# Order of work in the prologue, the first slice, the last attention and the closing sum of a fused attention and MLP kernel

## The chip, the cores and the metric

The kernel runs on one core of a Trainium2 chip. The metric is the device time of one execution in microseconds (us). TensorE is PE in the rows, VectorE DVE, ScalarE ACT, GpSimd POOL, and SyncE SP; "PEld" is TensorE's loading of weights, and a name with a q behind it (ACTq, SPq) is an engine's own queue of DMA issues.

## The reference

```python
def _attn_ref(q, k, v, lam):            # q, k, v: (4, 8, 768, 64)
    block = 64
    ...
    for b in range(nb):
        sl = slice(b * block, (b + 1) * block)
        qb, kb, vb = (q[:, :, sl], k[:, :, sl], v[:, :, sl])
        intra = np.einsum('bhic,bhjc->bhij', qb, kb) * Dmask[None]
        intra = np.einsum('bhij,bhjd->bhid', intra, vb)
        inter = np.einsum('bhid,bhde->bhie', qb * lam_pow[None], kv_state)
        out[:, :, sl] = intra + inter
        kb_dec = kb * rev_pow[None]
        kv_state = lam_block[None, :, None, None] * kv_state + np.einsum('bhsd,bhse->bhde', kb_dec, vb)
    return out

def _moe_ref(x, w_in, w_out):           # x: (3072, 512), d_ff 2048
    h = x @ w_in
    r = np.maximum(h, 0.0)
    g = r * r
    return g @ w_out
```

An attention with a decaying state, in order of the tokens, gives 3072 rows of 512; two matrix products with a squared ReLU between them follow.

## The kernel before

**Tiles and stages.** The tokens are cut into 24 chunks of 128 (`NT`), four batches of six; four chunks make a group of 512 tokens (`G`), so there are six groups. Of each group the MLP's hidden layer is made in 16 slices of 128 features (`NF`). The program runs through a prologue (chunks 0 to 3: loads, masks, their attention), then the first group's 16 slices beside the attention of chunks 4 to 7, then the second group's slices beside chunks 8 to 15, then the groups 2 and 3 in eight steps `quad` beside chunks 16 to 23, their gathering (`gather_all(2, ...)`), and the same for groups 4 and 5 (`quad_all`, `gather_all(4, ...)`). The order of the instructions on every engine is the order of the calls in the program: each engine has one queue and works it off in that order, waiting on semaphores.

**Two parts per number.** Products are made of a high and a low part (types of 32 bits): `wh`, `wl` for weights, `xh`, `xl` for activations, `gh`, `gl` for the squared hidden layer. A product of two numbers is three matmuls: high by high, low by high, high by low.

**A chunk of attention.** `scores(t)` makes k by q on TensorE, `masked(t)` multiplies them by the mask on VectorE (two instructions), `within(t, ...)` multiplies the result with v on TensorE, `news` and `faded` make the state's update, `update` writes the state `kv` (ScalarE up to chunk 3, VectorE behind), `before(t, ...)` adds the product of q and the state, `split` and the function that it returns write `xh` (ScalarE) and `xl` (VectorE). `prep_k` and `prep_q` multiply k and q by powers of lambda on POOL. In the prologue these calls are written out one by one.

**The weights of the first group.** The weights come as 64-bit words in 17 units (`NLOT`; unit u holds slice u of the first matrix and slice u - 1 of the second). A unit goes through a row of steps: `wload(u)` (SP, two DMAs into `raw`, of which there are two buffers), `first_hi(u)` (ScalarE, L120, absolute value into `A`, also two buffers) and `first_lo(u)` (ScalarE, L125), then on VectorE `clamp(u)` L133, `shift(u)` L137, `sign(u)` L144 and `rounded(u)` L150 (an add, which frees `raw`), then `upper(u)` (ScalarE, L156, writes `wh`) and `lower(u)` (VectorE, L159, writes `wl` and frees `A`). `turn(u, ...)` is a copy of one element on POOL that puts POOL's queue behind a step of VectorE. Slice f of the first group calls `hidden(0, f, ...)` first (12 matmuls, L518, which need unit f), then the steps of unit f + 2 (clamp to rounding add) and the last steps of unit f + 1, then `square` (ScalarE: a ReLU and two squares, L525 to L528) and `rest` (VectorE, L533, the remainder `gl` of slice f), and at last on TensorE `project` of the slice before, which needs `gh`, `gl` of that slice and unit f. The body of that loop:

```python
        h = hidden(0, f, *xs_of[0])
        if f < 3:
            ...
        else:
            if u_ < NLOT:
                for op in (clamp, shift, sign):
                    op(u_)
            if f > 3:
                upper(u_ - 1)
            lower(u_ - 1)
            ...
            if u_ < NLOT:
                rounded(u_)
        wload(u_ + 2)
        ...
        rest(0, f, h, gh)
        ...
        if step == 1 and f > 1:
            masked(t)
```

**Last attention.** In `quad(n)` seven products (`product(n, i, ...)`, six matmuls each, L691) run with one attention among them (`go`, L446 and others). `go` multiplies q by the old state, puts a one-element copy on ScalarE (`mark`, L462) behind it, on which the second half waits, runs what the caller gave it as `ahead` and the next chunk's scores, and then the rest. In the last step (n = 7) there is no next chunk, so nothing runs between the two halves.

**Closing sum.** `gather_all` multiplies the gathered rows into seven banks; in its last round it adds them in pairs on VectorE (`add`, L214) and stores four quarters of the output from ScalarE's queue (`put_out`, L1046).

Of the kernel before, what the change touches and what calls it, by code (L numbers as in the profile page):

```python
# [15 lines left out]
P = 128  # L16
# [9 lines left out]
G = 4  # L26
# [9 lines left out]
def body(ctx: ExitStack, tc: tile.TileContext, qT, kT, kvq, lam, w, out):  # L36
# [476 lines left out]
    def hidden(m, f, xh, xl):  # L513
        h = ps_h.tile([P, N], F32, name="h")
        k = 0
        for wt, x in ((wh, xh), (wl, xh), (wh, xl)):
            for kt in range(KT):
                nc.tensor.matmul(  # L518
                    h, wt[:, f, kt * P : (kt + 1) * P], x[:, kt], start=k == 0, stop=k == 11
                )  # L520
                k += 1
        return h
# [263 lines left out]
    def quad(n, prev, far_, last_):  # L786
# [9 lines left out]
        def attention():  # L796
            if n and n in FOLDED:
                fold_whole(FOLDED[n])
            go(t, None if last else t + 1, a_at)
            if t + 2 < NT:  # L800
                load_qk(t + 2)
                load_kv(t + 2)
            if n == NQ - 2:
                move(11, by_half(io.tile([P, 2 * DM], F32, name="qk_sb")[:, 0:DM]))
            if not last:
                scale_q(t + 1)
            if n == 3:
                E[6] = wk.tile([P, N], F32, name="kept", tag="a")
# [27 lines left out]
        product(n, 3, pb, False, False)  # L836
# [207 lines left out]
    def put_out(m, par, two, half, x):  # L1044
        o_ = out[m * G * C : (m + 2) * G * C].rearrange("(r s w p) d -> p r s w d", r=2, s=2, w=2)
        store = lambda: nc.scalar.dma_start(out=o_[:, :, two, par, half * 2 * P : (half + 1) * 2 * P], in_=x.rearrange("p (r d) -> p r d", r=2))  # L1046
# [5 lines left out]
    def gather_all(m, after):  # L1052
        for par in range(2):
# [8 lines left out]
            for n in range(NQ):  # L1062
                q = par * NQ + n
                end = n == NQ - 1
                for i in range(7):
# [21 lines left out]
                    if i == 3:  # L1087
                        add(u3, banks[3], u2)
                        add(o12[0][:, 0], banks[2], u3)
                        put_out(m, par, 1, 1, o12[0][:, 0])  # L1090
# [101 lines left out]
    low[1] = split(1, o[1])  # L1192
    scores(3, ps_acc, "acc")
# [3 lines left out]
    att(2, ps_a, "att")  # L1197
    news(2, u[2])
    faded(2, u[2])
    before(2, o[2], True, False)  # L1200
    update(2, u[2])
    within(2, o[2], False, True)
# [23 lines left out]
    for f in range(NF):  # L1226
        t, step, u_ = G + f // 4, f % 4, f + 2
        h = hidden(0, f, *xs_of[0])
        if f < 3:
# [9 lines left out]
            sign(u_)  # L1239
            if f != 1:  # L1240
                rounded(u_)
        else:
            if u_ < NLOT:
                for op in (clamp, shift, sign):
                    op(u_)
            if f > 3:
                upper(u_ - 1)
            lower(u_ - 1)
            if u_ - 1 < NF:
                turn(u_ - 1, False)  # L1250
            if u_ < NLOT:
                rounded(u_)
        wload(u_ + 2)
        if f == 3:
            low[G]()
# [15 lines left out]
        if f == 1:  # L1271
            rounded(u_)
        if step == 1 and f > 1:
# [176 lines left out]
```

## Time and profile before

| what | us |
|---|---|
| median of three runs (575.71 to 576.35) | 576.0 |
| the profiled execution | 575.8 |
| its span in the profile | 574.0 |
| TensorE busy (98%) | 565.0 |
| VectorE busy (77%) | 441.9 |
| ScalarE busy (52%) | 299.4 |
| POOL busy (17%) | 95.4 |

The times in the rows count from the span's start. A row of the timeline has start, length, engine, line and operation, output and inputs with their tile names, and in brackets how long the engine sat idle ahead of it and what released it. TensorE's matmuls overlap: a matmul of 128x512 has 0.39 us in its row, though the next starts 0.23 later. The first group's slices lie between 25.7 and 127 us, the last attention of `quad` at 324 to 328, the closing sum behind 565.

### The profile page before, as it was taken

To read this page: it belongs to the slowest core of one execution; us is meant where nothing else is said; L and a number is where in the kernel's file an instruction comes from. 1 tells how busy PE (TensorE), PEld (TensorE's weight loads), DVE (VectorE), ACT (ScalarE), POOL (GpSimd) and SP (SyncE) were. 2 spreads that over 40 slices of the span, in tenths; PEclk is the share of its full clock that TensorE was granted. 3 is DMA by queue.
4 is the path that set the end of the run, shared out by engine and by line. 5 is a ranking of instruction groups with operands and counts; after the bars stand their busy time and mean duration, and the time that the engine had idled before them with its cause. 6 is when DMAs were issued, how large, how long until landed. Compare 5 with 4: busy or idle time off the path is not lost.

```text
span 574.0 us, 13432 instructions
## 1 busy us (share of the span) xinstructions
PE 565.0 (98%) x5308; PEld 492.8 (86%) x5308; DVE 441.9 (77%) x732; ACT 299.4 (52%) x524; POOL 95.4 (17%) x107
## 2 busy tenths in 40 slices
PE   9998999999999999999999999999999999999996
PEld 7886888888888888888888799999988888999996
DVE  6899999987787667777773799696865457997933
ACT  4677877834555556566665775153423234541610
POOL 5430321432322233222433000000000000000000
PEclk9999999999999999999999999999999999999999
DMA  8947485427599887599999776799588766766863
GB/s 293 351 150 271 147 276 193 155 103 265 184 353 361 271 264 269 179 306 376 385 372 352 247 223 218 205 297 338 188 267 246 190 196 196 234 212 211 288 202 107
DMA packets 87325, 142.69 MB, mean 249 GB/s; under 512 B 7776, under 2 KB 40544, under 8 KB 87264
## 3 DMA queue, kind: packets, MB, share of 16 engines
q1 hardware_dynamic: 82624, 136.61, 72.2%
q10 hardware_dynamic: 4640, 5.24, 2.5%
q8 instruction: 42, 0.69, 0.5%
q14 instruction: 19, 0.16, 0.1%
HBM read 106.96 MB, written 31.46 MB: 241 GB/s over the span
## 4 chain that ended last, share of the span: by engine, by line
PE 87%; DMA 5%; DVE 5%; ACT 1%; issue 1%; SPq 1%; DVEq 0%; ACTq 0%
PE h L691 19%; PE acc L1035 16%; PE h L518 12%; PE att L1035 8%; PE att L691 8%; PE acc L549 4%; PE h L1035 4%; PE acc L554 4%; PE acc L550 4%; PE acc L446 2%; DMA lent<-in_qT 1%; PE att L446 1%; DMA ws<-parts 1%; DMA kv_sb<-in_kvq 1%; DMA qk_sb<-in_qT 1%
## 5 line engine op out<-in xcount | busy, mean ns | idle before, releaser
L691 PE MATMUL h<-wh,ring 128*128 128x512 f32 x320 | 87.1, 394 | 0.0
L691 PEld LDWEIGHTS h<-wh,ring 128*128 128x128 f32 x320 | 59.2, 188 | 13.3 <-DVE kv_sb L214 0.4
L1035 PE MATMUL acc<-folds,wh 128*128 128x256 f32 x384 | 70.5, 283 | 0.0
L1035 PEld LDWEIGHTS acc<-folds,wh 128*128 128x128 f32 x384 | 59.9, 192 | 0.0
L1007 ACT CAST wh<-sums 128x1024 fp32r<-128x1024 f32 x32 | 33.6, 1050 | 45.9 <-DVE sums L214 15.2
L1035 PE MATMUL acc<-folds,wl 128*128 128x256 f32 x192 | 54.3, 283 | 0.0
L549 PE MATMUL acc<-wh,gh 128*128 128x512 f32 x128 | 50.3, 393 | 0.0
L554 PE MATMUL acc<-wh,gl 128*128 128x512 f32 x128 | 49.9, 390 | 0.0
L550 PE MATMUL acc<-wl,gh 128*128 128x512 f32 x128 | 49.9, 390 | 0.0
L691 PE MATMUL h<-wl,ring 128*128 128x512 f32 x160 | 49.3, 390 | 0.0
L214 DVE TENSOR_TENSOR wl<-sums,wh 128x1024 fp32r<-128x1024 f32 x37 | 45.1, 1220 | 2.8 <-ACT wh L1007 2.8
L525 ACT ACTIVATE h<-h 128x512 f32<-128x512 f32 x32 | 18.7, 583 | 43.1 <-PE h L518 43.1
L1035 PEld LDWEIGHTS acc<-folds,wl 128*128 128x128 f32 x192 | 36.9, 192 | 0.0
L507 POOL TENSOR_TENSOR kvd<-kv,qpow 128x256 f32<-128x256 f32 x27 | 20.7, 766 | 96.7 <-DVE kv L214 79.6
L518 PE MATMUL h<-xh,wh 128*128 128x512 f32 x128 | 36.1, 403 | 0.0
L518 PE MATMUL h<-xh,wl 128*128 128x512 f32 x128 | 34.5, 392 | 1.5 <-DVE wl L159 1.5
L533 DVE TENSOR_TENSOR gl<-h,gh 128x512 fp32r<-128x512 f32 x32 | 22.0, 686 | 17.9 <-ACT h L528 17.9
L691 PEld LDWEIGHTS h<-wl,ring 128*128 128x128 f32 x160 | 30.0, 188 | 6.4
L691 PE MATMUL att<-wh,ring 128*128 128x512 f32 x128 | 34.3, 390 | 0.0
L518 PE MATMUL h<-xl,wh 128*128 128x512 f32 x128 | 34.3, 390 | 0.0
L518 PEld LDWEIGHTS h<-xh,wl 128*128 128x128 f32 x128 | 23.9, 188 | 7.2 <-DVE wl L159 1.9
L886 ACT ACTIVATE h<-h 128x512 f32<-128x512 f32 x16 | 9.3, 581 | 38.3 <-PE h L691 27.2
(267 smaller groups left out, 1423.9 us busy)
## 6 DMA issues: line engine op xcount, KB each, us to landing
folds<-wt SPq DMA_DIRECT2D x128, 256.0 KB, 3.8
ring<-ws SPq DMA_DIRECT2D x112, 256.0 KB, 4.1
raw<-in_w SPq DMA_DIRECT2D x30, 512.0 KB, 4.3
kv_sb<-in_kvq SPq DMA_DIRECT2D x22, 512.0 KB, 6.0
ws<-parts SPq DMA_DIRECT2D x32, 256.0 KB, 4.6
qk_sb<-in_kT SPq DMA_DIRECT2D x22, 256.0 KB, 4.6
qk_sb<-in_qT SPq DMA_DIRECT2D x22, 256.0 KB, 5.0
out_x<-qk_sb ACTq DMA_DIRECT2D x16, 256.0 KB, 5.1
```

What stands on the lines that cost most here:

```text
L214: lambda o, x, y, op=op: V.tensor_tensor(out=o, in0=x, in1=y, op=op)
L446: nc.tensor.matmul(o[h][r, p * D : (p + 1) * D], x, y, start=(h, r.start) not in begun, stop=end, skip_group_check=True,)
L507: nc.gpsimd.tensor_tensor(out=kvd, in0=d, in1=qpow[:, :, D - 1 : D].broadcast_to([P, NPR, D]), op=ALU.mult)
L518: nc.tensor.matmul(h, wt[:, f, kt * P : (kt + 1) * P], x[:, kt], start=k == 0, stop=k == 11)
L525: nc.scalar.activation(h, h, AF.Relu)
L533: V.tensor_tensor(out=gl, in0=r, in1=gh.bitcast(F32), op=ALU.subtract)
L549: nc.tensor.matmul(accs[m][i], gh[:, cs], wh[:, j], start=f == 0, stop=False)
L550: nc.tensor.matmul(accs[m][i], gh[:, cs], wl[:, j], start=False, stop=False)
L554: nc.tensor.matmul(accs[m][i], gl[:, cs], wh[:, j], start=False, stop=end)
L691: nc.tensor.matmul(bank, x[:, part_, kt], t[:, q + kt], start=start and z == 0, stop=stop and z == 5, skip_group_check=True,)
L1007: nc.scalar.copy(o_, x)
L1035: nc.tensor.matmul(bank[:, r * 2 * P : (r + 1) * 2 * P], x, y, start=k == 0 and r == 0 and z == 0, stop=k == NQ - 1 and z == 2, skip_group ...
```

## The change

- **Prologue.** The masked product of chunk 2 (`within(2, ...)`) now comes ahead of the scores of chunk 3; it opens the bank, and `before(2, ...)` closes it.
- **First group.** In slices 4 to 15 `hidden` takes the matmuls of `wl` last. In slices 0 to 5 the rounding add of unit f + 2 comes behind the remainder of slice f, and with it the load of unit f + 4; in slice 1 the sign step too. In slice 3 the lower weights of unit 4 come first, a marker stands behind unit 5's sign step, and `low[G]` comes behind the rounding add.
- **Last attention.** Product 3 of the last `quad` runs between the two halves of the attention.
- **Closing sum.** The first quarter is made by a ScalarE copy of bank 3 and a POOL add of `c` (bank 2 plus `u2`), and is stored from SP's queue; VectorE has one add less.

```diff
@@ hidden
-        for wt, x in ((wh, xh), (wl, xh), (wh, xl)):
+        order = ((wh, xh), (wl, xh), (wh, xl))
+        if m == 0 and f > 3:
+            order = order[0], order[2], order[1]
+        for wt, x in order:
@@ quad, attention()
-            go(t, None if last else t + 1, a_at)
+            if last:
+                go(t, None, a_at, ahead=(lambda: product(n, 3, pb, False, False), lambda: None))
+            else:
+                go(t, t + 1, a_at)
@@ quad
-        product(n, 3, pb, False, False)
+        if not last:
+            product(n, 3, pb, False, False)
@@ put_out
-    def put_out(m, par, two, half, x):
+    def put_out(m, par, two, half, x, queue=nc.scalar):
-        store = lambda: nc.scalar.dma_start(...)
+        store = lambda: queue.dma_start(...)
@@ gather_all
                     if i == 3:
                         add(u3, banks[3], u2)
-                        add(o12[0][:, 0], banks[2], u3)
-                        put_out(m, par, 1, 1, o12[0][:, 0])
+                        if m == 4 and par:
+                            nc.scalar.copy(o12[0][:, 0], banks[3])
+                            nc.gpsimd.tensor_tensor(out=o12[0][:, 0], in0=o12[0][:, 0], in1=c, op=ALU.add)
+                            put_out(m, par, 1, 1, o12[0][:, 0], nc.sync)
+                        else:
+                            add(o12[0][:, 0], banks[2], u3)
+                            put_out(m, par, 1, 1, o12[0][:, 0])
@@ prologue
+    att(2, ps_a, "att")
+    within(2, o[2], True, False)
     scores(3, ps_acc, "acc")
     prep_q(3)
     prep_k(3)
     masked(3)
-    att(2, ps_a, "att")
     news(2, u[2])
     faded(2, u[2])
-    before(2, o[2], True, False)
+    before(2, o[2], False, True)
     update(2, u[2])
-    within(2, o[2], False, True)
@@ the loop over the first group's slices
-            sign(u_)
             if f != 1:
-                rounded(u_)
+                sign(u_)
         else:
+            if f == 3:
+                lower(u_ - 1)
             if u_ < NLOT:
                 for op in (clamp, shift, sign):
                     op(u_)
-            if f > 3:
+            if f == 3:
+                turn(u_, True)
+            else:
                 upper(u_ - 1)
-            lower(u_ - 1)
-            if u_ - 1 < NF:
-                turn(u_ - 1, False)
-            if u_ < NLOT:
+                lower(u_ - 1)
+                if u_ - 1 < NF:
+                    turn(u_ - 1, False)
+            if 5 < f and u_ < NLOT:
                 rounded(u_)
-        wload(u_ + 2)
-        if f == 3:
-            low[G]()
+        if f > 5:
+            wload(u_ + 2)
...
         rest(0, f, h, gh)
         if f == 1:
+            sign(u_)
+        if f <= 5:
             rounded(u_)
+            wload(u_ + 2)
+        if f == 3:
+            low[G]()
```

VectorE, slices 0 and 1, from the clamp of unit 2 (buffer `A_413`) to the rounding add of unit 3 (`A_463`); `a_493`, `a_495` are the masked scores of chunk 4. Before:

```order
L144 SCALAR_TENSOR_TENSOR A_413<-raw_300,A_413 128x1024
L150 ISA A_413<-raw_300,A_413 128x2048
L533 TENSOR_TENSOR gl_460<-h_433,gh_457 128x512
L159 TENSOR_TENSOR wl_98<-A_413,wh_97 128x2x512
L133 TENSOR_SCALAR A_463<-A_463 128x1024
L137 TENSOR_SCALAR A_463<-A_463 128x1024
L304 TENSOR_TENSOR a_493<-att_466,mask_165 128x512
L304 TENSOR_TENSOR a_495<-att_467,mask_165 128x512
L144 SCALAR_TENSOR_TENSOR A_463<-raw_423,A_463 128x1024
L533 TENSOR_TENSOR gl_507<-h_476,gh_504 128x512
L150 ISA A_463<-raw_423,A_463 128x2048
```

Now:

```order
L144 SCALAR_TENSOR_TENSOR A_413<-raw_300,A_413 128x1024
L536 TENSOR_TENSOR gl_456<-h_433,gh_453 128x512
L150 ISA A_413<-raw_300,A_413 128x2048
L159 TENSOR_TENSOR wl_98<-A_413,wh_97 128x2x512
L133 TENSOR_SCALAR A_463<-A_463 128x1024
L137 TENSOR_SCALAR A_463<-A_463 128x1024
L304 TENSOR_TENSOR a_493<-att_466,mask_165 128x512
L304 TENSOR_TENSOR a_495<-att_467,mask_165 128x512
L536 TENSOR_TENSOR gl_503<-h_476,gh_500 128x512
L144 SCALAR_TENSOR_TENSOR A_463<-raw_423,A_463 128x1024
L150 ISA A_463<-raw_423,A_463 128x2048
```

The remainders (L533, now L536) have moved ahead of the rounding adds (L150), and in slice 1 ahead of the sign step (L144); between the rounding add of unit 2 and its lower weights (L159) nothing is left.

VectorE, slice 5, from the clamp of unit 7 (`A_680`) to the masked scores of chunk 5 (`a_735`, `a_737`); `A_636` is unit 6. Before:

```order
L133 TENSOR_SCALAR A_680<-A_680 128x1024
L137 TENSOR_SCALAR A_680<-A_680 128x1024
L144 SCALAR_TENSOR_TENSOR A_680<-raw_626,A_680 128x1024
L159 TENSOR_TENSOR wl_98<-A_636,wh_97 128x2x512
L150 ISA A_680<-raw_626,A_680 128x2048
L533 TENSOR_TENSOR gl_733<-h_705,gh_730 128x512
L304 TENSOR_TENSOR a_735<-att_695,mask_165 128x512
L304 TENSOR_TENSOR a_737<-att_696,mask_165 128x512
```

Now:

```order
L133 TENSOR_SCALAR A_680<-A_680 128x1024
L137 TENSOR_SCALAR A_680<-A_680 128x1024
L144 SCALAR_TENSOR_TENSOR A_680<-raw_632,A_680 128x1024
L159 TENSOR_TENSOR wl_98<-A_636,wh_97 128x2x512
L536 TENSOR_TENSOR gl_729<-h_705,gh_726 128x512
L150 ISA A_680<-raw_632,A_680 128x2048
L304 TENSOR_TENSOR a_735<-att_695,mask_165 128x512
L304 TENSOR_TENSOR a_737<-att_696,mask_165 128x512
```

The remainder of slice 5 and the rounding add of unit 7 have changed places; the mask is last in both.

TensorE in the prologue, from the masked product of chunk 1 to that of chunk 3 (`lent_111` holds chunk 2, `lent_118` chunk 3; L285 scores, L327 masked products, L334 products with the state). Before:

```order
L327 MATMUL acc<-a,kv_sb 64x128 x8
L285 MATMUL acc<-lent_118 128x128 x8
L319 MATMUL att<-lent_111 64x64 x8
L341 MATMUL att<-kv,fade 64x64 x8
L334 MATMUL att<-lent_111,kv 64x128 x8
L327 MATMUL att<-a,lent_111 64x128 x8
L334 MATMUL acc<-lent_118,kv 64x128 x8
L327 MATMUL acc<-a,lent_118 64x128 x8
```

Now:

```order
L327 MATMUL acc<-a,kv_sb 64x128 x8
L327 MATMUL att<-a,lent_111 64x128 x8
L285 MATMUL acc<-lent_118 128x128 x8
L319 MATMUL att<-lent_111 64x64 x8
L341 MATMUL att<-kv,fade 64x64 x8
L334 MATMUL att<-lent_111,kv 64x128 x8
L334 MATMUL acc<-lent_118,kv 64x128 x8
L327 MATMUL acc<-a,lent_118 64x128 x8
```

Chunk 2's masked product has left its place between the two products with the state and stands ahead of chunk 3's scores.

## Rows read from the trace of the kernel before

**Rows 1.** Waits of TensorE: engine, line, releaser: us in total, times, longest.

```profile
PE h L518 <- DVE wl L159: 1.5, 1, 1.5
...
PE acc L285 <- DMA lent<-in_qT: 1.3, 1, 1.3
PE acc L446 <- ACT mark L462: 0.3, 1, 0.3
```

**Rows 2.** A stretch: start:end, length, busy time of each engine, clock, DMA share, GB/s.

```profile
68.00:128.00 60.00, 60.00 (x390) 48.94 (x390) 56.97 (x72) 42.72 (x58) 17.40 (x19) 1.00 0.50 171
```

**Rows 3.** Chain of waits, slice 6: start, length, what.

```profile
63.26 2.72 PE h L518 x12
65.98 1.04 PE att L327 x14
```

**Rows 4.** Timeline of VectorE, slices 1 to 5.

```profile
33.38 1.23 DVE L159 TENSOR_TENSOR wl<-A,wh 128x1024 fp32r<-128x1024 f32 x1 [0.52 <-ACT wh L156]
...
38.79 1.70 DVE L150 CUSTOM_DVE_ANT_0 A<-raw,A 128x2048 uint16<-128x2048 uint16 x1
...
47.60 0.69 DVE L133 TENSOR_SCALAR A<-A 128x1024 f32<-128x1024 f32 x1 [0.76 <-ACT A L120]
...
57.51 1.22 DVE L150 CUSTOM_DVE_ANT_0 A<-raw,A 128x2048 uint16<-128x2048 uint16 x1
...
62.97 1.22 DVE L150 CUSTOM_DVE_ANT_0 A<-raw,A 128x2048 uint16<-128x2048 uint16 x1
64.11 0.68 DVE L533 TENSOR_TENSOR gl<-h,gh 128x512 fp32r<-128x512 f32 x1
64.71 1.28 DVE L304 TENSOR_TENSOR a<-att,mask 128x512 f32<-128x512 f32 x2
```

**Rows 5.** Timeline of ScalarE, slices 0, 2 to 3 and 5.

```profile
30.48 0.59 ACT L528 ACTIVATE h<-h 128x512 f32<-128x512 f32 x1
...
45.49 1.05 ACT L156 CAST wh<-A 128x1024 fp32r<-128x1024 f32 x1 [1.25 <-DVE A L150]
...
50.12 0.59 ACT L528 ACTIVATE h<-h 128x512 f32<-128x512 f32 x1
...
63.91 1.16 ACT L120 ACTIVATE A<-raw 128x1024 f32<-128x1024 f32 x1 [1.55 <-DMA raw<-in_w]
```

**Rows 6.** Timeline of POOL, the multiplies of q of chunks 4 and 5.

```profile
37.15 2.26 POOL L292 TENSOR_TENSOR qk_sb<-qk_sb,qpow 128x512 f32<-128x512 f32 x1
...
64.19 1.30 POOL L292 TENSOR_TENSOR qk_sb<-qk_sb,qpow 128x512 f32<-128x512 f32 x1
```

**Rows 7.** Timeline of all engines, prologue, chunks 2 and 3.

```profile
17.74 1.33 POOL L298 TENSOR_TENSOR lent<-lent,mask 128x512 f32<-128x512 f32 x1 [1.59 <-DMA lent<-in_kvq]
...
18.90 1.16 PE L285 MATMUL acc<-lent 64*128 64x128 f32 x16 [1.32 <-DMA lent<-in_qT]
...
22.10 0.76 ACT L351 COPY kv<-att 64x256 f32<-64x256 f32 x2 [3.05 <-PE att L334]
...
22.72 1.17 PE L334 MATMUL acc<-lent,kv 128*64 128x128 f32 x15
```

**Rows 8.** Timeline of TensorE, the three products behind the last attention.

```profile
325.77 1.21 PE L691 MATMUL h<-wh,ring 128*128 128x512 f32 x4
...
327.28 1.09 PE L691 MATMUL h<-wh,ring 128*128 128x512 f32 x4
...
328.67 1.07 PE L691 MATMUL h<-wh,ring 128*128 128x512 f32 x4
```

**Rows 9.** Timeline of the end: the four stores' issues, VectorE's last add.

```profile
568.94 2.17 ACTq L1046 DMA_DIRECT2D out_x<-qk_sb  x4
...
570.03 0.68 DVE L214 TENSOR_TENSOR qk_sb<-att,p 128x512 f32<-128x512 f32 x1
```

**Rows 10.** DMA from 560 to 574: busy tenths in 40 slices; issues, size, us to landing.

```profile
DMA  6874110000000000000000000000899999991000
...
out_x<-qk_sb ACTq DMA_DIRECT2D x4, 256.0 KB, 2.3
```

More of the change, by code (lines that the diff above doesn't have):

```diff
@@ L1042, in body @@
     held = []
-    def put_out(m, par, two, half, x):
+    def put_out(m, par, two, half, x, queue=nc.scalar):
         o_ = out[m * G * C : (m + 2) * G * C].rearrange("(r s w p) d -> p r s w d", r=2, s=2, w=2)
-        store = lambda: nc.scalar.dma_start(out=o_[:, :, two, par, half * 2 * P : (half + 1) * 2 * P], in_=x.rearrange("p (r d) -> p r d", r=2))
+        store = lambda: queue.dma_start(out=o_[:, :, two, par, half * 2 * P : (half + 1) * 2 * P], in_=x.rearrange("p (r d) -> p r d", r=2))
         if m == 2 and par:
```

## The prediction

> **What bounds the kernel.** I read the waits first. In 574.0 us TensorE has three waits in the middle of its work that name a releaser of this change: 1.5 us on VectorE's lower weights (`wl`, L159), 1.3 us on the load of the fourth chunk's q, 0.3 us on a small copy of ScalarE in the last attention [rows 1]. Each part of the change aims at one of them, the closing sum at the last adds. Then the stretches: from 68 to 128 us TensorE is busy 60.00 of 60.00 us [rows 2], and the waits name no later one before 300 us, so a delay or a gain on its way there is carried to the end one for one.
>
> Then the chain of waits at the end of that early stretch: TensorE leaves a first product at 65.98 (63.26 + 2.72) and starts the masked product of chunk 5 at 65.98 [rows 3]. VectorE's own rows say that the operand, the masked scores of chunk 5, is made from 64.71 to 65.99 [rows 4]. Both arrive together, so at that point VectorE has no slack, and what decides the first slice is not the 1.5 us wait but **when VectorE finishes that mask**. VectorE never waits for TensorE before it: its rows wait for ScalarE's casts and loads (0.52 at 33.38, 0.76 at 47.60) and one rounding add takes 1.70 instead of 1.22 [rows 4]. VectorE, ScalarE, POOL and the loads form a loop of their own that TensorE follows.
>
> **The change, part by part.** VectorE's instructions up to the mask are the same ones; only waits differ. So I count how much later than before VectorE comes, from unit to unit.
>
> *Unit 2.* The remainder of slice 0 now stands ahead of the rounding add. It needs ScalarE's third square, 30.48 + 0.59 = 31.07 [rows 5], so it starts at 31.1; a remainder takes 0.60 to the next start (64.11 to 64.71) [rows 4]; the add then runs 31.7 to 32.9 (1.22), ScalarE's cast takes 1.05 [rows 5], and the lower weights of unit 2 start at 34.05 against 33.38 [rows 4]. Before, the remainder filled this gap; now nothing does. **+0.67.**
>
> *Unit 3.* Before, POOL's multiply of chunk 4's q (37.15 to 39.41) [rows 6] stretched the rounding add by 0.48 [rows 4]. Now the sign step of unit 3 stands there instead, with the multiply also 0.67 later (it waits for unit 3's shift). Held up to the multiply's end it loses about 0.5, as before, and the rounding add follows its own sign step with no remainder between. I take **+0.25**; bounds 0 (nothing but the swap) and +0.6 (both held).
>
> *Units 4 and 5.* The 0.76 wait at 47.60 goes, since the lower weights of unit 4 now run while ScalarE prepares unit 5. In its place: those lower weights wait for their cast, 1.05 behind the rounding add, while VectorE has only the state's two adds: about 0.3. The remainder of slice 3 now comes ahead of the rounding add of unit 5 and needs seven ScalarE instructions that begin with the release by unit 4's rounding add, 45.49 to 50.12 + 0.59 = 5.22 us [rows 5]; VectorE has in that time the state's adds (some 0.9), the wait of 0.3 and the four steps that lie between a remainder and the next rounding add (62.97 less 57.51 + 1.14 + 0.60: 3.7) [rows 4], 4.9: so 0.3 to 0.4 of wait. With 0.1 more at slice 2's remainder, **-0.1**; bounds -0.76 (no new wait) and +0.4.
>
> *Unit 7.* Its words are loaded when the rounding add of unit 5 has freed the buffer, and that add is now one remainder and one wait later. For unit 8 before, the add ended at 57.51 + 1.22 = 58.73 [rows 4] and the load released ScalarE at 63.91 after 1.55 of idle [rows 5]: 5.18. The same 5.2, and then the absolute value (1.15), put the clamp of unit 7 some **+0.35** behind VectorE's readiness; bounds 0 and 0.6.
>
> *The mask.* In slice 5 the order is now lower weights of unit 6, remainder, rounding add of unit 7, mask. POOL multiplies chunk 5's q as soon as a marker on unit 6's lower weights lets it. Before, the rounding add (62.97 to 64.19) [rows 4] was first, and the multiply ran from 64.19 for 1.30 beside remainder and mask, which it did not stretch [rows 6]. Now the remainder is first, POOL starts in it, and the rounding add meets the multiply, as at 38.79. It is ready 0.6 after the remainder's start; the multiply ends some 1.6 after it: **+0.85**; bounds 0 (POOL comes second) and +1.0. Trainium skill, page SBUF — State Buffer, section Who interferes with whom: a VectorE instruction with two SBUF inputs and a GpSimd instruction that reads SBUF exclude each other for the whole instruction, and the one that issues first wins. By that the rounding add would start only at the multiply's end, +1.0 instead of 0.85; the 1.70 row agrees in kind, with somewhat less.
>
> Sum at the mask: 0.67 + 0.25 - 0.1 + 0.35 + 0.85 = **+2.0**. TensorE's 1.5 us wait does go, also by its order (wh on xh, wh on xl, wl on xh: the lower weights are needed 0.91 later, a third of 2.72 [rows 3]). But TensorE then stands at the masked product earlier, at about 65, and waits there near 3 us for a mask that ends at 68.0. Behind it both queues go on as before and 2.0 later. Ends: +0.3 (only unit 2 certain, the rest at the low bounds, part of -0.76) and +2.8.
>
> *Prologue.* TensorE waits 1.32 for q of chunk 3; V of chunk 2 lands 1.2 us earlier, when POOL goes on at 17.74 [rows 7], so the eight-pair masked product (L327) fits in. But the next thing on TensorE, chunk 3's product with the state, needs ScalarE's copies of the state, and these wait for chunk 2's product with the state (L334), which stands behind the awaited scores as before: 22.10 + 0.76 = 22.86 [rows 7]. Before, that product began at 22.72 and could not pass its second matmul until then. So the 0.9 us moved away leaves a wait on `kv`: **0**; bounds -0.15 (the row's 1.17 was stretched) and +0.15 (refilling after a wait).
>
> *Last attention.* The 0.27 wait [rows 1] goes behind a product that runs in it. But the large matmuls are entered twice: the product after attention takes 325.77 to 327.28 = 1.51, the next 327.28 to 328.67 = 1.39 [rows 8], so 0.12 more. ScalarE's copies out of the attention, and the casts behind them, come one product (1.4) later; TensorE had no wait on them [rows 1]. **-0.1**; bounds -0.3 and +0.3.
>
> *Closing sum.* VectorE loses one of its adds, the last starts when its bank is ready, 0.4 before 570.03 [rows 9]. One ScalarE copy, one POOL add and one store on SP run beside that. The row of these four stores says 2.3 us from issue to landing [rows 10]; by that row the end moves by -0.4. But the transfers are busy at 0.8 to 0.9 for eight slices of 0.35 us, 2.8 us without a gap [rows 10], and the first store is issued no earlier than the 568.94 of before [rows 9], since the add ahead of it still follows the same three. The same bytes from the same start end at the same time: **0**, bounds -0.4 and +0.1. Trainium skill, page DMA: Bandwidth & Descriptors, section Issuing engines are not separate DMA queues: DMAs of all issuing engines run on the same 16 DMA engines. By that rule a second queue gives 0; the busy slices agree.
>
> Sum: 2.0 + 0 - 0.1 + 0 = +1.9. The profiled execution took 575.8 us (574.0 of span); the median of the three runs is 576.0, 0.2 above, so the forecast for the median is **577.9 us**.
>
> **The rivals.** 0.2% is 1.15 us, about what a measurement of this kernel tells from no change.
>
> *VectorE keeps up (faster).* If the new order lets VectorE through without the new waits, TensorE gains what VectorE gains at the mask: the 0.76 wait and the 0.48 stretch, no more, since TensorE came at the very time of the mask. With the last attention 576.0 - 1.24 - 0.1 = 574.7 us. It decides if the mask of chunk 5 ends before 65 us. For it: ScalarE and POOL have much idle time; the 1.5 wait is real. Against it: the unit 2 step needs no assumption, the gap there has nothing to fill it.
>
> *Only the certain waits.* POOL's multiply and the rounding add miss each other, and unit 7's load is in time: 2.0 - 0.85 - 0.35 = +0.8, with -0.1 outside: 576.7 us. For it: who comes first is a matter of 0.3 us. Against it: the marker releases POOL just behind the lower weights, where VectorE's next is the remainder.
>
> *More than that.* A rounding add that comes 2 us or more later also frees later buffers later; if unit 8's or 9's load then holds ScalarE and VectorE once more, +3.1: 579.0 us. Against it: behind the mask VectorE's rows and the loads move together.
>
> That the change does nothing is the prologue's case, counted above at 0.
>
> **How the numbers follow.** Forecast 0.55, only the certain waits 0.25, VectorE keeps up 0.15, more 0.05. Faster by over 0.2%: 0.15; within: 0.25; slower: 0.60. Leaving out the 574.7 case and the upper one, the range goes from the low end of the certain waits with the low ends outside, 576.0 + 0.3 - 0.3 - 0.4 = 575.6, to the high end of the slice, 576.0 + 2.8 = 578.8.
>
> **What would show it.** In the changed profile the wait on L159 (1.5) should be gone from TensorE's list, and one of 2 to 3 us on VectorE's masked scores stand ahead of the masked product of chunk 5; the mask should start at about 66.7 instead of 64.71, the lower weights of unit 2 at 34.05, unit 7's rounding add take about 2 us. The q wait of the prologue should shrink to 0.3 with a new one of about 0.6 on `kv`; the 0.3 on the marker copy go; the last store land at the same distance from the last matmul. The prediction is wrong if the mask starts before 65.5, or if TensorE has a gap later in the slice that it has not now.

## The result and the profile after

The changed kernel takes **579.81 us** (median of 6 executions, 578.00 to 581.13) against 575.57 for the kernel before on the same chip (574.91 to 576.35). The ratio is **1.0066 [1.0053, 1.0079]**: 3.8 us slower by this ratio (the medians themselves differ by 4.2), where 1.9 was forecast, and outside the range. The profiled execution took 579.58, with a span of 577.8.

| what | before | after |
|---|---|---|
| span, profiled execution | 574.0 | 577.8 |
| mean granted TensorE clock | 0.998 | 0.997 |
| TensorE busy | 565.0 | 568.3 |
| VectorE busy | 441.9 | 443.8 |
| masked product of chunk 5 starts on TensorE | 65.91 | 67.56 |
| slice 7's first product starts | 70.79 | 74.50 |
| gathering starts | 331.38 | 334.96 |

TensorE's waits in the kernel after: the 1.5 on the lower weights, the 1.3 on q and the 0.3 on the marker of [rows 1] are gone. What stands in their place (us in total, times, longest):

```profile
PE att L327 <- DVE a L304: 2.2, 2, 2.0
...
PE acc L334 <- ACT kv L351: 0.6, 1, 0.6
PE acc L557 <- DVE gl L536: 0.5, 1, 0.5
```

The first row is the wait on the masked scores, the second the prologue's wait on the state. VectorE's timeline in the kernel after shows where the masked scores lost their time; compare each start with [rows 4] and, for the clamps, with these rows of the kernel before:

```profile
40.42 0.68 DVE L133 TENSOR_SCALAR A<-A 128x1024 f32<-128x1024 f32 x1
...
53.79 0.68 DVE L133 TENSOR_SCALAR A<-A 128x1024 f32<-128x1024 f32 x1
...
59.24 0.69 DVE L133 TENSOR_SCALAR A<-A 128x1024 f32<-128x1024 f32 x1
```

After:

```profile
34.00 1.22 DVE L159 TENSOR_TENSOR wl<-A,wh 128x1024 fp32r<-128x1024 f32 x1 [1.12 <-ACT wh L156]
...
41.33 0.69 DVE L133 TENSOR_SCALAR A<-A 128x1024 f32<-128x1024 f32 x1
...
54.65 0.68 DVE L133 TENSOR_SCALAR A<-A 128x1024 f32<-128x1024 f32 x1
...
60.45 0.69 DVE L133 TENSOR_SCALAR A<-A 128x1024 f32<-128x1024 f32 x1 [0.25 <-ACT A L120]
...
64.78 2.12 DVE L150 CUSTOM_DVE_ANT_0 A<-raw,A 128x2048 uint16<-128x2048 uint16 x1
66.83 1.27 DVE L304 TENSOR_TENSOR a<-att,mask 128x512 f32<-128x512 f32 x2
```

Lower weights of unit 2 at 34.00 (33.38 before), clamps of units 4, 6 and 7 at 41.33, 54.65 and 60.45 (before 40.42, 53.79, 59.24), and the mask at 66.83 (64.71): VectorE is 0.62, 0.91, 0.86, 1.21 and at last 2.12 late. This much the prediction has. What it doesn't have is in TensorE's own rows behind the wait. Before:

```profile
65.91 1.11 PE L327 MATMUL att<-a,kv_sb 128*64 128x128 f32 x15
...
66.94 1.06 PE L334 MATMUL att<-qk_sb,kv 128*64 128x128 f32 x15
67.93 0.50 PE L549 MATMUL acc<-wh,gh 128*128 128x512 f32 x1
...
70.79 1.07 PE L518 MATMUL h<-xh,wh 128*128 128x512 f32 x4
```

After:

```profile
67.56 0.43 PE L327 MATMUL att<-a,kv_sb 128*64 128x128 f32 x2 [2.05 <-DVE a L304]
68.16 0.98 PE L327 MATMUL att<-a,kv_sb 128*64 128x128 f32 x13 [0.16 <-DVE a L304]
...
68.98 1.88 PE L334 MATMUL att<-qk_sb,kv 128*64 128x128 f32 x15
70.79 0.79 PE L552 MATMUL acc<-wh,gh 128*128 128x512 f32 x1
71.38 0.63 PE L553 MATMUL acc<-wl,gh 128*128 128x512 f32 x1
...
74.50 1.07 PE L521 MATMUL h<-xh,wh 128*128 128x512 f32 x4
```

The product with the state takes 1.88 for 15 matmuls (1.06 before), a 128x512 matmul 0.63 (0.39 before). The stretches of the same execution (columns as in [rows 2]; the clock is the third number from the end):

```profile
65.50:67.50 2.00, 0.02 (x1) 0.00 (x0) 2.00 (x3) 2.00 (x3) 0.33 (x1) 1.00 0.00 0
...
68.90:72.40 3.50, 3.50 (x26) 2.88 (x22) 3.47 (x4) 2.06 (x5) 0.44 (x1) 0.55 0.67 268
```

Narrower stretches show where the clock changes:

```profile
67.60:69.20 1.60, 1.44 (x21) 1.20 (x23) 1.56 (x3) 1.57 (x3) 0.00 (x0) 1.00 0.72 125
69.20:72.60 3.40, 3.40 (x20) 2.75 (x17) 3.37 (x4) 1.99 (x4) 0.64 (x1) 0.50 0.63 254
```

TensorE stands idle for 2 us, works 1.6 us at full clock, and then has 1.2 GHz instead of 2.4 (0.50) for 3.4 us. Half of that stretch is lost, **1.7 us**. The rows agree: from the product with the state to the second products it takes 1.81 (68.98 to 70.79) where it took 0.99 (66.94 to 67.93), and from there to slice 7 3.71 where it took 2.86, so 0.82 + 0.85 = 1.67 more for the same matmuls. In the kernel before the clock is 1.00 there.

So of TensorE's 3.71 us at the next slice (74.50 less 70.79) some 2.0 are the late mask (1.65 at its start, the rest until the masked product has its second half and runs on) and 1.7 the clock. The other places: last attention 331.38 - 324.18 = 7.20 before, 334.96 - 327.90 = 7.06 after, -0.14. At the end the adds are done earlier, the stores not:

```profile
572.63 1.84 ACTq L1053 DMA_DIRECT2D out_x<-qk_sb  x3
...
572.65 1.28 POOL L1098 TENSOR_TENSOR qk_sb<-qk_sb,p 128x512 f32<-128x512 f32 x1 [248.36 <-ACT qk_sb L1097]
...
573.34 0.69 DVE L214 TENSOR_TENSOR qk_sb<-att,p 128x512 f32<-128x512 f32 x1
573.96 0.39 SPq L1053 DMA_DIRECT2D out_x<-qk_sb  x1
```

The last add starts 3.31 later than in [rows 9], so 0.4 earlier than the rest of the program; the first store is issued 3.69 later and the span ends 3.8 later. The 0.4 is not worth anything, as reckoned.

### The profile page after: what moved, and what is told of

Read it like the earlier page. It is cut to its first block, busy times and chain, and to the rows that moved or that the text cites. A ratio compares the mean times of both kernels' runs of the same rounds, so it can differ in the third digit from the quotient of the medians.

```text
span 577.8 us, 13441 instructions
## 1 busy us (share of the span) xinstructions
PE 568.3 (98%) x5308; PEld 493.9 (85%) x5308; DVE 443.8 (77%) x731; ACT 299.8 (52%) x525; POOL 93.2 (16%) x108
## 4 chain that ended last, share of the span: by engine, by line
PE 90%; DVE 4%; ACT 3%; DMA 1%; issue 1%; POOL 1%; SPq 0%; POOLq 0%; ACTq 0%
PE h L694 19%; PE acc L1042 16%; PE h L521 12%; PE att L1042 8%; PE att L694 8%; PE acc L552 4%; PE acc L553 4%; PE acc L557 4%; PE h L1042 4%; PE att L446 2%; PE acc L446 2%; DVE A L150 1%; PE att L327 1%; DMA raw<-in_w 1%; PE h L411 1%; PE att L426 1%
## 5 line engine op out<-in xcount | busy, mean ns | idle before, releaser
L528 ACT ACTIVATE h<-h 128x512 f32<-128x512 f32 x32 | 18.7, 584 | 48.3 <-PE h L521 48.3
L1098 POOL TENSOR_TENSOR qk_sb<-qk_sb,p 128x512 f32<-128x512 f32 x1 | 1.3, 1276 | 248.4 <-ACT qk_sb L1097 248.4
L536 DVE TENSOR_TENSOR gl<-h,gh 128x512 fp32r<-128x512 f32 x32 | 22.0, 687 | 19.1 <-ACT h L531 19.0
L552 PEld LDWEIGHTS acc<-wh,gh 128*128 128x128 f32 x128 | 24.3, 189 | 6.3 <-ACT gh L530 0.7
```

Of the source, the lines that this page charges most:

```text
L528: nc.scalar.activation(h, h, AF.Relu)
L536: V.tensor_tensor(out=gl, in0=r, in1=gh.bitcast(F32), op=ALU.subtract)
L552: nc.tensor.matmul(accs[m][i], gh[:, cs], wh[:, j], start=f == 0, stop=False)
```

## The experiments

The theory, formed on these rows: the loss is VectorE's lateness as predicted, plus a fall of TensorE's clock that the wait brings about. Rivals: another part of the change has its share; the fall has nothing to do with the wait; only the mask matters, or VectorE's lateness costs time anyway.

**Which part of the change.** The first-group part alone, and all but the first-group part:

```diff
@@ the kernel before: hidden and the loop over the slices as changed, nothing else
+        order = ((wh, xh), (wl, xh), (wh, xl))
+        if m == 0 and f > 3:
+            order = order[0], order[2], order[1]
...
+        if f <= 5:
+            rounded(u_)
+            wload(u_ + 2)
```

> The kernel before with the first-group part alone (VectorE's order in slices 0 to 5, lower weights last). Theory A (late mask, then a lower clock): the whole loss stands at the mask of chunk 5: TensorE waits about 2 us for masked scores that begin at 66.8, and behind the wait its granted clock falls for some 4 us; 579 to 580 us, single executions without the fall 577.9. Rival B (the other parts have a share of it): 577 to 578.5 in the median, with the rest in the other kernel of this call.

Measured: 578.88 us, ratio 1.0051 [1.0034, 1.0068]. That lies between the ranges of the two theories. Its profile has the same wait (2.05, ended at 67.47) and the same fall of the clock, which here begins with the end of the wait and not 1.6 us behind it:

```profile
65.50:67.30 1.80, 0.00 (x0) 0.00 (x0) 1.80 (x2) 1.80 (x3) 0.24 (x1) 1.00 0.00 0
67.40:70.70 3.30, 3.23 (x28) 2.92 (x30) 3.23 (x6) 2.48 (x4) 0.00 (x0) 0.50 0.86 271
```

Three of its five executions have a mean clock of 0.996 or 0.997, the other two 0.999 and 1.000.

```diff
@@ the changed kernel: hidden and the loop over the slices as before
-        order = ((wh, xh), (wl, xh), (wh, xl))
...
-        if f <= 5:
-            rounded(u_)
-            wload(u_ + 2)
```

> The changed kernel with the first-group part undone: prologue, last attention and closing sum alone. Theory A: 575.2 to 575.7 against 575.6, no wait on the marker copy, a wait of about 0.6 on the state in the prologue, lower weights of L159 waited for as before (1.5). Rival B: 577 or more, the loss in the last attention or at the end. Rival C (these parts gain what the clock hides in the changed kernel): 575.0 or less.

Measured: 576.1 us, ratio 1.0001 [0.9991, 1.0010]. The median lies 0.4 above the range expected, but the interval includes 1. So the loss is in the first group, as far as these runs can tell; prologue, last attention and closing sum together are no difference that they show.

**Is it the wait that brings the clock down?** First attempt to keep TensorE at work in the wait:

```diff
@@ attend
+        if t == G + 1:
+            for k in range(8):
+                nc.tensor.matmul(o, wh[:, 6, ...], xs_of[0][0][:, k % KT], start=True, stop=True)
         within(t, o, True, not t % NCB)
```

> The changed kernel with eight matmuls of 128x512 more on TensorE (their result is overwritten by the masked product of chunk 5) in the place where it waits for the masked scores of chunk 5. Theory A (the pause brings the clock down): the mask is as late as before, but the clock stays at 1.00 from 66 to 78 and the time is 577.5 to 578.0, with little scatter. Rival (the fall of the clock has nothing to do with the pause): 579.5 to 580, a stretch below 1.00 as in the changed kernel.

Measured: 582.61 us, 1.0116 [1.0092, 1.0141]. A miss of the experiment, not of the theory: the timeline of TensorE shows the added matmuls behind the wait, since their bank is freed by the mask itself, and most of them run at half clock (3.14 for eight, which take 1.99 at full clock in the second attempt's profile below):

```profile
68.28 3.14 PE L372 MATMUL att<-xh,wh 128*128 128x512 f32 x8 [2.05 <-DVE a L304]
```

It adds work and leaves the pause, so it says nothing on a filled wait. But it is one more kernel with a pause of 2.05, and four of its six executions have a mean clock of 0.996 or less. Its profile, with 0.992, even has a second fall, behind another wait of TensorE:

```profile
490.86 1.20 PE L699 MATMUL h<-wh,ring 128*128 128x512 f32 x4 [1.79 <-DVE kv_sb L214]
```

```profile
492.40:495.60 3.20, 3.20 (x9) 2.52 (x8) 2.95 (x5) 3.20 (x6) 0.00 (x0) 0.50 0.49 184
```

The second attempt takes another bank:

```diff
@@ attend
+        if t == G + 1:
+            early.append(ps_h.tile([P, N], F32, name="h"))
+            for k in range(8):
+                nc.tensor.matmul(early[0], wh[:, 6, ...], xs_of[0][0][:, k % KT], start=True, stop=True)
@@ hidden
-        h = ps_h.tile([P, N], F32, name="h")
+        h = early.pop() if early else ps_h.tile([P, N], F32, name="h")
```

> The changed kernel with eight matmuls of 128x512 more on TensorE, this time into the bank of slice 7's hidden layer, which is free by then (in the first attempt they went into the bank of the masked product and had to wait for the mask themselves). Theory A (the pause brings the clock down): they run from 65.4 to 67.3 inside the wait, the wait shrinks to under 0.5, the mask still begins near 66.8, the clock stays at 1.00, and the time is 577.3 to 578.0. Rival (the fall of the clock is not tied to the pause): 579.5 or more with a stretch below 1.00.

Measured: 579.27 us, 1.0070 [1.0057, 1.0082]. The time is a miss, the clock is as expected. TensorE's timeline and the stretch that had 0.55:

```profile
65.40 1.99 PE L375 MATMUL h<-xh,wh 128*128 128x512 f32 x8
67.62 0.43 PE L327 MATMUL att<-a,kv_sb 128*64 128x128 f32 x2 [0.24 <-DVE a L304]
...
69.04 1.14 PE L334 MATMUL att<-qk_sb,kv 128*64 128x128 f32 x15
```

```profile
68.90:72.40 3.50, 3.50 (x32) 2.93 (x29) 3.46 (x4) 2.00 (x4) 0.38 (x1) 1.00 0.68 265
```

With TensorE at work in the wait, the clock stays at 1.00 though the mask is as late (66.89), and the products behind it start 2.18 us after those of the kernel before (70.11 against 67.93) instead of 2.86. But this execution loses 0.58 at 281.9, where TensorE has a gap without a named cause, and 1.4 us much later, in the second quad stage, where TensorE waits for VectorE and VectorE's first sum has a gap that no wait explains. With the 2.2 that makes 4.2 of the 4.3 by which its span is longer (578.3 against 574.0):

```profile
485.19 0.42 DVE L214 TENSOR_TENSOR sums<-kept 128x256 f32<-128x256 f32 x1 [1.34 <-issue]
...
487.40 1.19 PE L702 MATMUL h<-wh,ring 128*128 128x512 f32 x4 [1.41 <-DVE kv_sb L214]
```

The same kernel once more, to see if that is scatter:

> The changed kernel with the eight matmuls in slice 7's bank, once more. Its first profile kept the clock at 1.00 up to 128 us and was 2.2 behind there, but lost 1.4 more at 487 where VectorE's first sum had 1.34 us without a named cause. If that is scatter of the single execution, this profile lacks it or has another size, and the span is 576.0 to 576.8. If it belongs to this order of work, it is there again with 1.2 to 1.5 and the span is 577.3 to 578.3.

Measured: 580.45 us, 1.0073 [1.0053, 1.0093]; the profiled execution is the fastest of the six (578.89, span 577.1). The gap is there again, as it is in the first attempt's profile (1.73), and it is not in the two profiles of the changed kernel, so it goes with the eight matmuls:

```profile
484.01 0.43 DVE L214 TENSOR_TENSOR sums<-kept 128x256 f32<-128x256 f32 x1 [1.23 <-issue]
```

Why it stands there was not tried. It spoils the time of this kernel as a price of the wait alone. Its clock can be used: in 11 of 11 executions the mean is 0.998 or more.

**Does every execution of the changed kernel pay the clock?**

> The changed kernel itself once more, to see how its executions scatter and for a second profile. If the fall of the clock behind the wait on the mask is what some executions pay and others not: those with a mean clock of 0.998 or more take 577.7 to 578.5, those below 0.998 579.3 to 580.5; the wait on the masked scores is 1.9 to 2.2 in the profile either way. Rival (every execution pays the same 3.8): no such split, 579.4 to 580.0 whatever the clock.

Measured: 578.67 us (577.47 to 581.28, nine executions), 1.0051 [1.0033, 1.0069]; wait 2.1, and in the profile:

```profile
66.00:72.00 6.00, 3.87 (x33) 3.37 (x32) 5.93 (x7) 4.41 (x6) 0.37 (x1) 0.72 0.53 176
```

They split. With the first six there are 15 executions of the changed kernel: **7 with a mean clock of 0.995 to 0.997**, median 579.58, and **8 with 0.999 or 1.000**, median 578.15. In 59 executions of the kernel before that ran beside these experiments the mean is never under 0.998. So the fall comes in about half of the executions, and costs 1.4 by these medians, 1.7 by the profile. Those without it are 2.6 above the 575.6 of before, where the forecast had 1.9; one of the eight, at 580.04 with a clock of 1.000, lost its 2 us elsewhere, and no profile shows where.

**The terms of the sum, undone.** Unit 7's rounding add ahead of the remainder again, as before:

```diff
-            if 5 < f and u_ < NLOT:
+            if 4 < f and u_ < NLOT:
                 rounded(u_)
...
-        if f > 5:
+        if f > 4:
             wload(u_ + 2)
...
-        if f <= 5:
+        if f <= 4:
             rounded(u_)
```

> The changed kernel with unit 7's rounding add ahead of slice 5's remainder again, as in the kernel before; slices 0 to 4 as changed. By the term of the mask (0.85) it should begin at 65.9 to 66.0 and TensorE wait 1.1 to 1.2 us. Theory A1 (a pause of this size leaves the clock alone, as the 1.52 of the kernel before did): 576.3 to 576.9. Theory A2 (any pause there brings the clock down): 578.3 to 579.

Measured: 577.32 us, 1.0034 [1.0021, 1.0046]. The rounding add takes 1.22 again, and the mask starts 2.87 behind the lower weights of unit 6 (66.55 less 63.68), against 3.78 in the changed kernel (66.83 less 63.05): 0.91 saved. This execution was 0.63 late at those lower weights already, from the prologue on (slice 0 begins at 26.41, in the changed kernel at 25.71), which is why the mask starts at 66.55 and not at 65.9. TensorE waits

```profile
67.28 0.43 PE L327 MATMUL att<-a,kv_sb 128*64 128x128 f32 x2 [1.14 <-DVE a L304]
```

which is the 2.05 of the changed kernel less the 0.91, and the clock is 1.00; no one of the five executions is under 0.998. The clock is as by theory A1; the median is 0.4 above its range. In the profile the late prologue accounts for that: at 136 us TensorE is 1.85 behind the kernel before, 1.17 without the 0.68 that it was behind at slice 0 (26.41 less 25.73). What the other executions had there isn't known.

Slices 0 and 1 as before:

```diff
-            if f != 1:
-                sign(u_)
+            sign(u_)
+            if f == 0:
+                rounded(u_)
+                wload(u_ + 2)
...
-        if f == 1:
-            sign(u_)
-        if f <= 5:
+        if 0 < f <= 5:
             rounded(u_)
```

> The changed kernel with slices 0 and 1 as in the kernel before (rounding adds of units 2 and 3 and the sign step ahead of the remainders or between as there); slices 2 to 15 as changed. By the terms of units 2 and 3 (0.67 + 0.25) the lower weights of unit 2 are back at 33.4, the mask begins at 65.8 to 66.0 and TensorE waits about 1.1: 576.5 to 577.3, no fall of the clock. Rival (what is lost in slices 0 and 1 is made up before the mask anyway): the mask still begins at 66.5 or later, 578 or more.

Measured: 578.36 us, 1.0043 [1.0027, 1.0059]: a miss, and the most telling one. VectorE does what was expected (lower weights of unit 2 at 33.65, 0.52 behind them as before; mask at 66.27, with 0.27 from the prologue):

```profile
33.65 1.22 DVE L159 TENSOR_TENSOR wl<-A,wh 128x1024 fp32r<-128x1024 f32 x1 [0.52 <-ACT wh L156]
...
66.27 1.27 DVE L304 TENSOR_TENSOR a<-att,mask 128x512 f32<-128x512 f32 x2
```

But TensorE loses its waits in slice 4 (0.5 and 0.2 in the changed kernel) too, begins slice 6 at 61.87, 1.23 us earlier than in the kernel before, and waits as long as ever:

```profile
PE att L327 <- DVE a L304: 2.2, 2, 2.1
```

and all six executions have a mean clock of 0.996 or 0.997: here the clock falls every time. The longest wait is 2.05 in the timeline, to the hundredth that of the changed kernel, although mask and TensorE both come 0.56 earlier. The loads of slice 6's weights (PEld) say why. In the changed kernel, and then in this one:

```profile
62.45 0.76 PEld L521 LDWEIGHTS h<-xh,wh 128*128 128x128 f32 x4 [0.42 <-ACT wh L156]
64.32 0.77 PEld L521 LDWEIGHTS h<-xh,wl 128*128 128x128 f32 x4 [0.18 <-DVE wl L159]
```

```profile
61.86 0.77 PEld L521 LDWEIGHTS h<-xh,wh 128*128 128x128 f32 x4 [0.49 <-ACT wh L156]
63.75 0.76 PEld L521 LDWEIGHTS h<-xh,wl 128*128 128x128 f32 x4 [0.20 <-DVE wl L159]
```

TensorE's slice 6 itself waits for unit 6's weights, which come out of VectorE's chain. What VectorE gains or loses ahead of them moves TensorE's arrival as much as the mask; by these rows the wait is set by what VectorE does between those lower weights and the mask. That also fits the kernel above: it saved 0.91 there, and the wait went from 2.05 to 1.14.

**Is it the mask alone?** The mask of chunk 5 ahead of unit 7's rounding add:

```diff
+        if f == 5:
+            masked(t)
         if f <= 5:
             rounded(u_)
...
-        if step == 1 and f > 1:
+        if step == 1 and f > 5:
             masked(t)
```

> The changed kernel with the masked scores of chunk 5 ahead of unit 7's rounding add. Theory A: the mask begins at about 64.8 (64.71 in the kernel before), TensorE waits under 0.3 us there, no fall of the clock, 575.2 to 575.9. Rival (VectorE's lateness of 2 us comes out in a later wait of TensorE: lower weights of unit 7, remainders of slices 6 to 9): a new wait behind 70 us and 576.5 to 578.

Measured: 577.31 us (575.94 to 579.17), 1.0023 [1.0011, 1.0036], a time of the rival. The mask starts at 64.68, TensorE is 0.03 ahead of the kernel before when it leaves the attention (67.90 against 67.93), no fall. But then it falls behind in small steps, +0.10 at 82, +0.51 at 116, +0.67 at 136, and in this execution it has a gap without a named cause in the quad stage:

```profile
316.06 0.27 PE L426 MATMUL acc<-kv_sb 64*64 64x64 f32 x2 [1.14 <-issue]
```

And the second products of slice 5 ahead of the masked product:

```diff
+        if f == 6:
+            project(*prev)
         if step == 2:
             low[t] = attend(t, ps_a, "att")
...
-        if prev is not None:
+        if prev is not None and f != 6:
             project(*prev)
```

> The changed kernel with the second products of slice 5 (twelve matmuls, 2.72 us) ahead of the masked product of chunk 5 on TensorE: work of the kernel itself fills the wait. Theory A: mask as late as before (66.8), TensorE gets to the masked product at about 68.2 without a wait, no fall of the clock; neither the 1.65 nor the 2.0 is paid, 575.0 to 576.0. Rival (VectorE's 2 us come out in the next slices as waits of TensorE): new waits of 1 to 2 us on lower weights or remainders between 70 and 90, 576.5 to 578.

Measured: 577.42 us, 1.0036 [1.0024, 1.0048]: the rival. The masked product starts without a wait at 68.60, the clock is 1.00, and slice 7 starts 0.30 before that of the kernel before; then TensorE loses 1.9 us up to 136 (+0.87 at 82, +1.58 at 136; 0.57 of it was there at slice 0, which begins at 26.30), in pieces of which the view of waits names none over 0.2, while VectorE is busy nearly throughout:

```profile
78.00:84.00 6.00, 5.92 (x35) 4.10 (x35) 5.93 (x8) 4.69 (x6) 1.13 (x2) 1.00 0.93 329
```

So VectorE's lateness is paid at the mask or, in part, behind it. By the ratios these two kernels are 1.3 and 2.1 above the kernel before, where the changed kernel without the fall is 2.6: keeping TensorE from the wait saves the clock, and a part of the lateness at most.

**The wait that the change aimed at.** The kernel before with the lower weights last, alone:

```diff
-        for wt, x in ((wh, xh), (wl, xh), (wh, xl)):
+        order = ((wh, xh), (wl, xh), (wh, xl))
+        if m == 0 and f > 3:
+            order = order[0], order[2], order[1]
+        for wt, x in order:
```

> The kernel before with the lower weights last on TensorE in slices 4 to 15 and nothing else. Theory: the wait on L159 goes from 1.5 to about 0.6, TensorE comes to the masked product of chunk 5 at about 65.0, where the first half of the mask is done at 65.4; it waits 0.4 there, so 0.3 to 0.5 is gained: 574.9 to 575.4 against 575.4 (no difference that these runs can tell). Rival (the 1.5 us wait was on the path that sets the end): 574.0 to 574.6.

Measured: 575.37 us, 0.9996 [0.9985, 1.0006]. The time is as expected, the waits are not quite: the wait of 1.5 splits into two in the same slice, and there is none at the mask, where 0.4 was expected:

```profile
PE acc L557 <- DVE gl L536: 0.8, 1, 0.8
PE h L521 <- DVE wl L159: 0.7, 1, 0.7
```

**What could be kept.** Lower weights of unit 4 ahead of unit 5's clamp and the lower weights last, all rounding adds as before:

```diff
@@ the loop of the kernel before; hidden and the other parts as changed
         else:
+            if f == 3:
+                lower(u_ - 1)
             if u_ < NLOT:
                 for op in (clamp, shift, sign):
...
-            lower(u_ - 1)
+            if f > 3:
+                lower(u_ - 1)
...
-        if f == 3:
-            low[G]()
...
+        if f == 3:
+            low[G]()
```

> Of the first-group part only two pieces are kept: lower weights of unit 4 ahead of unit 5's clamp, and the lower weights last on TensorE; all rounding adds and the sign step stand as in the kernel before; the other parts as changed. If the loop of VectorE, ScalarE and loads is the bound, the 0.76 wait goes without a new one: the mask begins at 63.9 to 64.1, TensorE is 0.65 ahead at the masked product, no wait over 0.3 in slices 3 to 6, and the time is 574.6 to 575.3 against 575.6. Rival: another wait (load of unit 7, remainder of slice 3) takes the 0.76 and the time is 575.5 to 576.

Measured: 575.50 us, 1.0003 [0.9994, 1.0011]. In the profile the loop gains what it should, though TensorE still has a wait of 0.67 on slice 4's remainder (at 52.56), where none over 0.3 was expected:

```profile
63.95 1.28 DVE L304 TENSOR_TENSOR a<-att,mask 128x512 f32<-128x512 f32 x2
```

The mask is 0.76 earlier, TensorE leaves the attention 0.76 earlier and gathers 0.92 earlier, and the span is 573.2 against 574.0 (573.5 in the profile of the other parts alone). The medians don't show it; the 59 executions of the kernel before lie 3.5 us apart (574.7 to 578.2). No kernel tried beats the kernel before by more than these runs can tell.

## Why the prediction was right or wrong

**VectorE's sum was right, term by term.** Unit 2: +0.67 predicted, +0.62 measured (34.00 less 33.38). Unit 3: +0.25, +0.29 (41.33 less 40.42 is 0.91). Units 4 and 5: -0.1 (its own pieces, 0.3 + 0.35 + 0.1 - 0.76, give 0.0), -0.05 (0.86). Unit 7: +0.35, +0.35 (1.21). Mask: +0.85, +0.91 (2.12). Sum +2.0 against +2.12, and the rounding add of unit 7 took 2.12 as expected.

**Prologue, last attention, closing sum were right.** A wait of 0.6 on the state in place of the q wait, -0.14 for -0.1, nothing at the end. The kernel with these alone shows no difference beyond its noise.

**The step that failed** is the sentence "Behind it both queues go on as before and 2.0 later". They don't: TensorE came to the mask at 65.5, waited 2.05, and in 7 of 15 executions then worked 3.4 us at half clock, 1.7 us in the profile. The prediction named the wait ("near 3 us", too long, since unit 6's weights held TensorE until 62.45) and asked only what it costs by itself; the clock stood in its sum at nothing, without a reason. That clock would have been a rival with about one chance in two. The kernel before offered a hint on the wrong side: its wait of 1.5 [rows 1] passed with a clock of 1.00, which says nothing on a longer one. The Trainium skill, page TensorE: Matmul & The Clock Gate, section Part 1: The HAM clock gate (the "warmup" mystery), says that the throttled state is the default and that activity releases the throttle; the trace agrees (1.00, then 0.50 behind the pause, then 1.00 again at work), and by that rule a step that exchanges a wait for a longer one asks for the clock as well.

**A size that was off.** Without the fall the changed kernel is 2.6 above the kernel before, for 1.9 forecast. "Both arrive together" was not exact: before, the first half of the mask was done at 65.35 (64.71 + 0.64), some 0.5 ahead of TensorE, so a mask 2.12 late makes the masked product 1.65 late. But its matmuls then wait for the second half as well and start up anew, and the products behind it are 2.18 late even where the wait is filled and the clock stays. With -0.14 from the last attention that is +2.0, what was forecast; the rest of the 2.6, about half a microsecond of the medians, isn't settled. The prologue may have a part in it: in the eleven profiles with the new prologue slice 0 begins between 25.47 and 26.50, in the three with the old one between 25.12 and 25.73.

The rival "more than that" gave 579.0, but by later loads that hold VectorE again; no such wait is in the rows. The chance of 0.6 for slower was on the right side; the range ended at 578.8 since the clock was not in it. The high bounds of its own terms add up to 3.3, not to the 2.8 that it took, but 579.3 would still have been too low.

## What to carry to other kernels

When a change moves a wait on TensorE, add up what the new wait makes of the clock: a pause that is longer than any in the old profile is a price of its own, to be read in the granted clock of the stretch behind it, and it may hit only some executions. And when an engine ahead of TensorE is busy nearly all the time, its lateness is paid wherever TensorE meets it; filling or moving the wait saved the clock here and only a part of the lateness. Look also at what lets TensorE come to the wait: where that hangs on the same late engine, a gain ahead of both leaves the wait as long as it was. Reordering gains only where it takes a gap out of that engine's row without opening another.

## What the runs showed of the hardware

- The clock of TensorE fell to half about pauses of 2.05 us, in some executions of three kernels (7 of 15, 3 of 5 and 4 of 6) and in all of another (6 of 6), and once behind a pause of 1.79. It did not fall in the 11 executions in which that wait was filled, in the 5 with a pause there of 1.14, nor in the 59 of the kernel before, with a pause of 1.52 in its profile. The low stretch took 3.4 us in the changed kernel's profile; it began 1.6 us after work had begun again there, and with the end of the pause in another kernel's profile.
- A gap of 1.2 to 1.7 us named "issue", with no wait, stood on VectorE at the same instruction in the three profiles of the kernels with eight matmuls more, and in neither of the changed kernel's two; one of 1.14 stood on TensorE in another kernel. They are of the size of the effects measured here, and their cause was not tried.
- A rounding add that met POOL's multiply (64.54 to 65.83) took 2.12 instead of 1.22, 0.90 more, where a wait to the multiply's end would have made it 1.05 (64.78 to 65.83). Of the prediction's two values for it, 0.85 by the rows and 1.0 by the rule that the Trainium skill, page SBUF — State Buffer, section Who interferes with whom, states, the first is nearer to the 0.91 by which the mask moved, but the two lie too close for one case to tell.
